# Both output accumulators in one PSUM bank, a quarter of a V chunk kept in the freed bank, and a shorter row norm in a two-layer attention decode kernel

## The chip, the cores and the metric

The kernel runs on one core of a Trainium2 chip. The metric is the device time of the launch in microseconds. The runs of the kernel before have a median of 1104.42 us (13 runs, 1099.99 to 1107.93); a run that was profiled took 1100.99 us.

## The reference, cut to what matters

Two layers are applied twice, with the same weights and the same caches in both passes. Layer A is attention of one new token per row over a cache; layer B is a small MLP. With a single position (S = 1) the four shifted groups of layer B are all zero, so its first two matrices drop out and only the part with `w3` and `w4` counts.

```python
B, Sq, D = 8, 1, 448;  Hq, Hkv, Sk, Dh = 16, 8, 4096, 256;  F = 1792    # bf16
# layer A
q = layernorm(x) @ wq                                  # 16 heads of 256
p = softmax(q . k_cache * Dh ** -0.5)                  # k_cache, v_cache: [8, 8, 4096, 256]
x = x + (p . v_cache) @ wo
# layer B, S = 1
y = layernorm(x);  x = x + y + gelu(layernorm(y) @ w3) @ w4
# ... then both layers once more
```

The caches hold 8 rows x 8 heads x 4096 x 256 x 2 bytes = 134 MB each. Pass 1 needs a query that depends on the end of pass 0 of the same row, so what isn't kept on the chip is read twice.

## The kernel before, in words

**Chunks and slots.** A task is one pass `ps` of one row `b` and one pair `gp` of key/value heads (4 pairs). It has four K chunks and four V chunks of 1 MB (128 partitions x 8 KB). SBUF has `NC = 15` places for chunks (`slots`). All chunk loads are issued on SP's queue by `emit_loads` (L671; L647 for two neighbouring K chunks at once), in the order in which the chunks are used, each as soon as a place is free. The engine that read a place last frees it: TensorE after the scores for K, TensorE after the product with the probabilities for V.

**What is kept.** Between a row's pass 0 and its pass 1, eleven chunks stay in their places (`kept`: all K of pairs 2 and 3, V chunks 1 to 3 of pair 3), so four of the 15 places are left for streaming. One more V chunk, `inner` (pair 2, V chunk 1), is saved in four PSUM banks: VectorE moves it as 128x512 uint32 transposes into `store` (`away`, L719) and later back into a place (`back`, L726). These twelve chunks of each row are loaded once only. The tasks are written out so that a row's two kept pairs come late in its pass 0, other rows' chunks stream while its chain runs, and pass 1 starts with the kept pairs.

**One chunk's work.** `items` is the hand-written order: K chunks of a task, interleaved with the V chunks of the task before it. For a K chunk VectorE transposes it in place (`transpose_k`, L684, three instructions), TensorE forms the scores into PSUM bank `sc` (L699), ScalarE takes the exponential (L708). `transpose_p` turns the probabilities (TensorE L735, ScalarE copy to `ptw` L742). For a V chunk `pv` (L754) adds 16 matmuls of 256 columns to an output accumulator in PSUM, one of two banks `o_banks`; `in_use` lists those taken. An accumulator serves two pairs of heads, then is drained.

**Side work.** The small work of a row is cut into generators, and the main loop calls `step` twice for each item, once ahead of the item's scores or `pv` and once at the item's end. `step` advances the first generator of each of three kinds in proportion to how far the item index is towards its due index.

- `half` drains an accumulator: sums of the exponentials (`z_cols`, VectorE L398 and L401, TensorE L409, VectorE L412), fold matrix `R` (L429), ScalarE copy of the accumulator to SBUF (L435), two small matmuls (L440), VectorE copy to `OT` (L444).
- `first_half` (pass 0, pairs 0 and 1) is `half` and the first part of the output projection (`add_cols`, L336). `chain` (pass 0, pairs 2 and 3) is `half`, the second part, the two additions to the residual `xT` (L465, L466), the MLP of the row (`mlp`, `norm` with `twice` set) and the query of pass 1 (`project_q`, `norm` again). `spread_q` then writes the query into a spread layout (L310).
- `first_last` and `last` drain pass 1. The last row's pairs 0 and 1 use another way (`pv_cols`), and the MLP of pass 1 is done for four rows at a time (`norm` with nb = 4).

`norm` for one row runs VectorE steps L210 to L224, one or two additions of epsilon (L245, L248), a power on GpSimd (L237), the centring (L251), and three scalings that write the bf16 operand `xb` (L262). The last 64 of the 448 features lie in the upper half of the partitions: `w3` and `wq` are stored with that tail split in two column halves, and `wblk` picks column 3 or 4 of `xb` for them.

PSUM has eight banks: `misc` (small results of many kinds at different columns), `sc`, two accumulators, four `store` banks.

Of the kernel before, what the change touches and what calls it, by code (L numbers as in the profile page):

```python
# [13 lines left out]
EPS = 1e-5  # L14
# [3 lines left out]
def kernel(  # L18
# [44 lines left out]
    kept = [(gp, 0, n) for gp in (GP - 1, GP - 2) for n in range(4)]  # L63
    kept += [(GP - 1, 1, n) for n in range(1, 4)]
    inner = (GP - 2, 1, 1)

    consts = ctx.enter_context(tc.tile_pool(name="consts", bufs=1))
    work = ctx.enter_context(tc.tile_pool(name="work", bufs=2))
# [43 lines left out]
    misc = psum.tile([128, 512], FP32, name="misc")  # L112
    ot_bank = misc[:, 256:320]
    sc = psum.tile([128, 512], FP32, name="sc")
    o_banks = [psum.tile([128, 512], FP32, name=f"o{n}") for n in range(2)]
    store = [psum.tile([128, 512], FP32, name=f"store{n}") for n in range(4)]
    for t in [sc] + o_banks:
        nc.vector.memset(t[:], 0.0)

    def room_ps(what, nb):  # L120

# [15 lines left out]
    ones = one[:].to_broadcast([128, 128])  # L137
    HTw = consts.tile([128, HC, Bn], BF16, name="HTw")
    nc.vector.memset(HTw[:], 0.0)
    nhalf = consts.tile([128, 1], FP32, name="nhalf")  # L140
    nc.vector.memset(nhalf[:], -0.5)
    xb = {}
# [29 lines left out]
    def wblk(t, cols, c, fc):  # L172

        if fc < 3:
            return t[:, fc * cols + 128 * c : fc * cols + 128 * c + 128], fc
        half = cols // 2
        if 128 * c < half:
            return t[:, 3 * cols + 128 * c : 3 * cols + 128 * c + 128], 3
        return t[:, 3 * cols + 128 * c - half : 3 * cols + 128 * c - half + 128], 4

# [12 lines left out]
    def norm(x, nb, twice):  # L193

        def room(name, shape, at):
            n = shape[0] * shape[1]
            if nb < Bn:
                t = chn.tile([128, n * MID], FP32, tag=name)  # L200
                ap = t[:, 0 : n * nb]
            else:
                ap = scratch(at, n * nb)
            return ap.rearrange("p (s f b) -> p s f b", s=shape[0], f=shape[1])

        def bc(ap):
# [36 lines left out]

        if twice:
            nc.vector.tensor_scalar(ve[:, 1], var, 0.0, EPS * EPS / (1 + EPS), ALU.max, ALU.add)  # L245
            if nb > 1:
                power(1, 2)
        nc.vector.tensor_scalar(ve[:, 0], var, 0.0, EPS, ALU.max, ALU.add)  # L248
        power(0, 2 if twice and nb == 1 else 1)
# [7 lines left out]
        parts = ((0, 128, 0, 0, 3, 0), (0, 64, 64, 3, 4, 3), (64, 128, 64, 3, 4, 4))  # L257
# [165 lines left out]
    def half(o_ps, zall, g8, OT):  # L423


        rz = yield from z_cols(zall, range(2 * g8, 2 * g8 + 2))

        R = chn.tile([128, 8], FP32, tag="R")
        nc.vector.tensor_mul(  # L429
            R[:].rearrange("p (g n) -> p g n", n=4),  # L430
            rz[:].rearrange("p n g -> p g n"),
            fold[:].rearrange("p (g n) -> p g n", n=4),
        )
        o_sb = chn.tile([128, Dh], FP32, tag="o_sb")
        nc.scalar.copy(o_sb[:], o_ps[:, 0:Dh])  # L435
        in_use.remove(o_ps)
        yield
        ot_ps = ot_bank[:, 32 * g8 : 32 * g8 + 16].rearrange("p (j h) -> p j h", j=2)
        for j in range(2):
            nc.tensor.matmul(  # L440
                ot_ps[:, j], o_sb[:].rearrange("p (i j) -> p j i", j=2)[:, j], R[:], start=True, stop=True
            )
        yield
        nc.vector.tensor_copy(OT[:, :, 8 * g8 : 8 * g8 + 8], ot_ps)  # L444
        yield
# [3 lines left out]
    def first_half(b, st):  # L449

        OT = work.tile([128, 2, Hq, 1], BF16, tag="OT", bufs=1)
        st["OT"] = OT
        yield from half(st["o", 0], st["z"], 0, OT[:, :, :, 0])
        yield from add_cols(
            y_room(1)[:, 0], lambda i: OT[:, i % 2, i // 2], wo_sb, range(NB2 // 2), 1
        )

    def chain(b, st):
        OT = st["OT"]
        yield from half(st["o", 1], st["z"], 1, OT[:, :, :, 0])  # L460
        yield from add_cols(
            y_room(1)[:, 1], lambda i: OT[:, i % 2, i // 2], wo_sb, range(NB2 // 2, NB2), 1
        )
        xs = xT[:, :, b : b + 1]
        nc.vector.tensor_add(xs, xs, y_room(1)[:, 0])  # L465
        nc.vector.tensor_add(xs, xs, y_room(1)[:, 1])  # L466
        yield from mlp(b, 1)
        qT = chn.tile([128, NB2], BF16, tag="qT2", bufs=2)
        yield from project_q(b, 1, qT[:].unsqueeze(2))
        state[1, b] = {"qT": qT}  # L470
# [75 lines left out]
    def inside(it):  # L546
        n, kv, c = it
        return (tasks[n][2], kv, c) == inner

    loads = [it for it in items if not (tasks[it[0]][0] == 1 and (stays(it) or inside(it)))]  # L550


# [79 lines left out]
    def emit_loads(most=None):  # L632
        n = 0
        while loads and places and n != most:
# [33 lines left out]
            else:  # L668
                src = rows.rearrange("(p x y) d -> x p (y d)", x=4, y=16)[c]
            if loads:  # L670
                nc.sync.dma_start(dst[:], src)  # L671
            else:
                for y in range(2):
                    nc.sync.dma_start(
# [69 lines left out]
            pt_ps.rearrange("p t k (a h) -> p a (t k) h", a=4),  # L744
        )

    def pv(o_ps, v, a, gp, begin):


        g = 2 * gp + a // 2  # L750
        for y in range(16):
            q = y % 4
            at = 128 * a + 8 * (4 * q + y // 4) + 6 - 2 * (g % 4)
            nc.tensor.matmul(  # L754
                o_ps[32 * q : 32 * q + 8, 0:256],
                ptz[:, at : at + 8],
                v[:, y * Dh : (y + 1) * Dh],
                start=(begin and y < 4),
                stop=(y >= 12),
                skip_group_check=True,  # L760
            )
# [39 lines left out]
            except StopIteration as e:  # L801
                return e.value

    gens, pairs_done, p_of, begun = [], {}, {}, set()
# [25 lines left out]
    for idx, it in enumerate(items):  # L830
# [65 lines left out]
        else:  # L896
# [23 lines left out]
            else:  # L920
                g8 = gp // 2
                if ("o", g8) not in st:
# [4 lines left out]
                pv(st["o", g8], slot, c, gp, begin=(ps, b, g8) not in begun)  # L927
                begun.add((ps, b, g8))
# [12 lines left out]
        if not (ps == 0 and stays(it)):  # L941
            if (ps, gp, kv, c) == (1, keep[-1], 0, 0):
                kept_place = p
            else:
                places.append(p)
        emit_loads()
        step(idx)
    while gens:
# [65 lines left out]
```

## Time and profile before

| what | value |
|---|---|
| median of 13 runs | 1104.42 us (1099.99 to 1107.93) |
| the profiled execution | 1100.99 us, span 1099.1 us |
| DMA | 448.90 MB, mean 408 GB/s |
| TensorE busy | 681.7 us (62%), granted clock 0.587 |
| VectorE busy | 586.3 us (53%) |
| ScalarE busy | 124.4 us (11%) |
| GpSimd busy | 16.3 us (1%) |
| chunk loads | 223 V of 1024 KB and 2 of 512 KB; 146 K of 1024 KB and 23 of 2048 KB |
| accumulators drained (L435) | 31 |

The busy shares are means over the whole span. The profile also gives the span in 40 slices of 27.5 us, the waits of each engine with what ended them, and a timeline; "SPq" in it is a DMA issue on SP's queue, and the text after "<-" in square brackets is what ended the engine's idle time before that row. All tables of stretches count from the span's start.

### The profile page before, as it was taken

What the parts mean: (1) busy time and instruction counts of PE and PEld (TensorE: products, weight loads), DVE (VectorE), ACT (ScalarE), POOL (GpSimd) and SP (SyncE); (2) the same over time, 40 slices, a digit from 0 to 9 for tenths busy, and PEclk for the clock granted to TensorE, in tenths of its full rate; (3) what the DMA queues carried; (4) which work ended last, traced back from release to release, by engine and by line L of the source; (5) the groups of instructions that cost most, each with busy time, mean ns of one, the idle gap of its engine ahead of it and who ended that gap; (6) DMA issues with size and microseconds to landing.
All of it is one profiled execution on the core that took longest, in us unless ns stands there. A gap on an engine that the chain in (4) does not pass through costs nothing. (4 is left out here: it accounts for less than half of the span.)

```text
span 1099.1 us, 32833 instructions
## 1 busy us (share of the span) xinstructions
PE 681.7 (62%) x15062; PEld 456.0 (41%) x15062; DVE 586.3 (53%) x1188; ACT 124.4 (11%) x362; POOL 16.3 (1%) x27
## 2 busy tenths in 40 slices
PE   3235668556864577446774477744777467867775
PEld 2123345334642355324542245522454245635554
DVE  5255564646356554556455564565637463576462
ACT  0001101110110011101020000200111101111110
POOL 0000000000000000000000000000000000000000
PEclk9996555655565556655565555755555555565575
DMA  9999999999999999999999999999999999999994
GB/s 361 396 426 420 419 397 420 420 413 409 417 423 420 405 416 422 424 419 398 419 422 422 421 399 418 423 422 415 409 419 421 419 405 420 421 414 403 417 418 186
DMA packets 62010, 448.90 MB, mean 408 GB/s; under 512 B 6568, under 2 KB 10544, under 8 KB 11312
## 3 DMA queue, kind: packets, MB, share of 16 engines
q1 hardware_dynamic: 61680, 446.42, 98.5%
q8 instruction: 118, 1.93, 0.7%
q10 hardware_dynamic: 192, 0.38, 0.1%
q14 instruction: 20, 0.16, 0.0%
HBM read 446.77 MB, written 0.01 MB: 407 GB/s over the span
## 5 line engine op out<-in xcount | busy, mean ns | idle before, releaser
L684 DVE STREAM_TRANSPOSE places<-places 128x512 uint32<-128x512 uint32 (+1 forms) x576 | 462.1, 858 | 282.3 <-DMA places<-in_A_k_cache_dram 274.1
L699 PE MATMUL sc<-places,qbd 128*8 128x128 bf16 (+1 forms) x6720 | 286.1, 313 | 226.3 <-DVE places L684 187.4
L754 PE MATMUL o<-places,ptw 128*8 128x256 bf16 x3968 | 246.3, 393 | 133.8 <-DMA places<-in_A_v_cache_dram 125.2
L699 PEld LDWEIGHTS <-qbd 128*8 128x8 bf16 x6720 | 164.4, 103 | 323.6 <-issue 146.7
L754 PEld LDWEIGHTS <-ptw 128*8 128x8 bf16 x3968 | 114.0, 111 | 181.4 <-issue 138.3
L708 ACT ACTIVATE p_n<-sc 128x256 bf16<-128x256 f32 x128 | 95.7, 748 | 806.0 <-PE sc L699 806.0
L287 PEld LDWEIGHTS <-wq_sb 128*128 128x128 bf16 x1152 | 35.9, 104 | 27.2 <-issue 18.9
L336 PEld LDWEIGHTS <-wo_sb 128*128 128x128 bf16 x1280 | 38.5, 103 | 19.7 <-issue 19.7
L310 DVE CAST qbd<-misc 32x64 bf16<-32x64 f32 x64 | 13.8, 216 | 55.8 <-PE misc L306 55.1
L287 PE MATMUL misc<-xb,wq_sb 128*128 128x1 bf16 x1024 | 34.5, 166 | 6.7 <-DVE xb L262 3.3
L336 PE MATMUL misc<-OT,wo_sb 128*128 128x1 bf16 x1024 | 34.4, 166 | 0.0
L708 ACT ACTIVATION_READ_ACCUMULATOR p_n<-sc 128x1 f32 x128 | 33.8, 264 | 0.0
L742 ACT CAST ptw<-misc 128x128 bf16<-128x128 f32 x64 | 17.5, 273 | 135.5 <-PE misc L735 75.8
L440 PEld LDWEIGHTS misc<-R,o_sb 128*128 128x128 f32 x124 | 28.0, 312 | 10.8 <-issue 8.7
L440 PE MATMUL misc<-R,o_sb 128*128 128x8 f32 x124 | 30.6, 358 | 0.4 <-ACT o_sb L435 0.3
L237 POOL TENSOR_TENSOR t<-t,nhalf 128x2 f32<-128x2 f32 (+2 forms) x20 | 14.0, 703 | 1069.5 <-DVE t L251 1069.5
L409 PE MATMUL misc<-zm,one 128*128 128x8 f32 (+1 forms) x66 | 18.1, 348 | 15.8 <-DVE zm L401 15.3
L726 DVE STREAM_TRANSPOSE places<-store 128x512 uint32<-128x512 uint32 x32 | 20.1, 685 | 11.3 <-PE sc L699 11.3
L409 PEld LDWEIGHTS misc<-zm,one 128*128 128x128 f32 x66 | 15.6, 293 | 22.1 <-issue 13.5
L354 PEld LDWEIGHTS <-w_sb 128*128 128x128 bf16 x560 | 17.2, 105 | 9.6 <-issue 9.4
L354 PE MATMUL misc<-xb,w_sb 128*128 128x1 bf16 (+1 forms) x560 | 18.5, 166 | 3.6 <-DVE xb L264 2.2
L719 DVE STREAM_TRANSPOSE store<-places 128x512 uint32<-128x512 uint32 x32 | 20.0, 694 | 1.0 <-DMA places<-in_A_v_cache_dram 0.9
(93 smaller groups left out, 227.3 us busy)
## 6 DMA issues: line engine op xcount, KB each, us to landing
places<-in_A_v_cache_dram SPq DMA_DIRECT2D x223, 1024.0 KB, 9.4
places<-in_A_k_cache_dram SPq DMA_DIRECT2D x146, 1024.0 KB, 10.7
places<-in_A_k_cache_dram SPq DMA_DIRECT2D x23, 2048.0 KB, 19.7
wo_sb<-in_A_wo_dram SPq DMA_DIRECT2D x1, 3584.0 KB, 28.5
wq_sb<-in_A_wq_dram SPq DMA_DIRECT2D x3, 1024.0 KB, 7.3
w_sb<-in_B_w_dram SPq DMA_DIRECT2D x1, 1568.0 KB
w_sb<-in_B_w_dram SPq DMA_DIRECT2D x3, 448.0 KB, 27.2
places<-in_A_v_cache_dram SPq DMA_DIRECT2D x2, 512.0 KB, 18.8
```

Of the source, the lines that this page charges most:

```text
L287: nc.tensor.matmul(q_ps[:, j * Hq + h, :], w, xbs(nb)[:, xi, :], start=(fc == 0), stop=(fc == 3),)
L336: nc.tensor.matmul(y_ps[:, fc, :], w[:, i, at : at + 128], rhs(i), start=start, stop=stop, skip_group_check=open is not None,)
L354: nc.tensor.matmul(h_ps[:, c * nb : c * nb + nb], w, xbs(nb)[:, xi, :], start=(fc == 0), stop=(fc == 3),)
L409: nc.tensor.matmul(z_ps, ones, zm[:], start=True, stop=True)
L440: nc.tensor.matmul(ot_ps[:, j], o_sb[:].rearrange("p (i j) -> p j i", j=2)[:, j], R[:], start=True, stop=True)
L684: nc.vector.transpose(w, w)
L699: nc.tensor.matmul(sc[32 * k : 32 * k + 8, 128 * x : 128 * (x + nx)], qbd[:, ep, gp].rearrange("p a h -> p (a h)"), v, start=(n == 0), sto ...
L708: nc.scalar.activation(p_sb[:, :, :, 2 * u : 2 * u + 2].rearrange("p t i x -> p x t i"), sc[:, 256 * u : 256 * u + 256].rearrange("p (x t ...
L719: nc.vector.transpose(store[n][:].bitcast(U32), slot[:].bitcast(U32)[:, 512 * n : 512 * n + 512])
L726: nc.vector.transpose(slot[:].bitcast(U32)[:, 512 * n : 512 * n + 512], store[n][:].bitcast(U32))
L742: nc.scalar.copy(ptw[:, :, :, 6:8], pt_ps.rearrange("p t k (a h) -> p a (t k) h", a=4),)
L754: nc.tensor.matmul(o_ps[32 * q : 32 * q + 8, 0:256], ptz[:, at : at + 8], v[:, y * Dh : (y + 1) * Dh], start=(begin and y < 4), stop=(y >= ...
```

## The change

1. **One bank for both accumulators.** `o0` and `o1` become the two halves (256 columns each) of one bank `o`. `pv` no longer starts its sum with the start flag. A matmul with zeros clears the whole bank at the beginning, and in `half` a VectorE memset clears the drained half after ScalarE's copy.
2. **A fifth store bank.** It keeps the first quarter (128 x 1024 bf16 = 2 KB per partition) of V chunk 0 of pair 3 (`part`). In pass 0 VectorE transposes it into the bank after the chunk's `pv`; in pass 1 VectorE transposes it back into the chunk's place one item ahead of its use, and the load of that chunk leaves the first quarter out.
3. **Shorter norm for one row.** With `twice` the two additions of epsilon are one instruction on two columns; in both kinds the first two of three scalings are one instruction with a constant mask `low`. For this, columns 3 and 4 of `xb` change roles, also in `wblk`.
4. **A moved addition.** The first of the two residual additions goes from `chain` to the end of `first_half`.

```diff
+    part = (GP - 1, 1, 0)
+    Q4 = 4 * Dh
...
-    o_banks = [psum.tile([128, 512], FP32, name=f"o{n}") for n in range(2)]
-    store = [psum.tile([128, 512], FP32, name=f"store{n}") for n in range(4)]
-    for t in [sc] + o_banks:
-        nc.vector.memset(t[:], 0.0)
+    o_both = psum.tile([128, 512], FP32, name="o")
+    o_banks = [o_both[:, 0:Dh], o_both[:, Dh : 2 * Dh]]
+    store = [psum.tile([128, 512], FP32, name=f"store{n}") for n in range(5)]
+    nc.vector.memset(sc[:], 0.0)
+    nc.tensor.matmul(o_both[:], ptz[:, 0:128], ptz[:, 0:512], start=True, stop=True)
...
+    low = consts.tile([128, 2, 4], FP32, name="low")
+    for k, v in enumerate((1.0, (1 + EPS) ** -0.5)):
+        nc.vector.memset(low[:, k], v)
+        nc.vector.memset(low[0:64, k, 3:4], 0.0)
+    eps2 = consts.tile([128, 2], FP32, name="eps2")
+    nc.vector.memset(eps2[:, 0:1], EPS)
+    nc.vector.memset(eps2[:, 1:2], EPS * EPS / (1 + EPS))
...
-        if twice:
-            nc.vector.tensor_scalar(ve[:, 1], var, 0.0, EPS * EPS / (1 + EPS), ALU.max, ALU.add)
-            if nb > 1:
+        if twice and nb == 1:
+            nc.vector.scalar_tensor_tensor(
+                ve[:, :, 0], var.to_broadcast([128, 2]), 0.0, eps2[:], ALU.max, ALU.add
+            )
+            power(0, 2)
...
+        if nb == 1:
+            nc.vector.scalar_tensor_tensor(
+                xbs(1)[:, 0:4, 0], xc[:, :, 0], rl, low[:, int(twice)], ALU.mult, ALU.mult
+            )
+            parts = parts[1:2]
...
-        nc.scalar.copy(o_sb[:], o_ps[:, 0:Dh])
-        in_use.remove(o_ps)
+        nc.scalar.copy(o_sb[:], o_ps)
+        nc.vector.memset(o_ps, 0.0)
+        in_use[:] = [t for t in in_use if t is not o_ps]
...
+        xs = xT[:, :, b : b + 1]
+        nc.vector.tensor_add(xs, xs, y_room(1)[:, 0])
...
-        nc.vector.tensor_add(xs, xs, y_room(1)[:, 0])
...
-                nc.sync.dma_start(dst[:], src)
+                z0 = Q4 if tasks[t][0] == 1 and halfway(it) else 0
+                nc.sync.dma_start(dst[:, z0:], src[:, z0:])
...
-                start=(begin and y < 4),
+                start=False,
...
+                if ps == 0 and halfway(it):
+                    nc.vector.transpose(store[4][:].bitcast(U32), slot[:, 0:Q4].bitcast(U32))
...
+        soon = items[idx + 1] if idx + 1 < len(items) else it
+        if tasks[soon[0]][0] == 1 and halfway(soon):
+            nc.vector.transpose(
+                slots[where[soon]][:, 0:Q4].bitcast(U32), store[4][:].bitcast(U32)
+            )
```

`halfway(it)` is true for the item that `part` names.

More of the change, by code (lines that the diff above doesn't have):

```diff
@@ L177, in wblk @@
         if 128 * c < half:
-            return t[:, 3 * cols + 128 * c : 3 * cols + 128 * c + 128], 3
-        return t[:, 3 * cols + 128 * c - half : 3 * cols + 128 * c - half + 128], 4
+            return t[:, 3 * cols + 128 * c : 3 * cols + 128 * c + 128], 4
+        return t[:, 3 * cols + 128 * c - half : 3 * cols + 128 * c - half + 128], 3
     def rows_to_cols(row, nb):
@@ L242, in power @@
             )
-        if twice:
-            nc.vector.tensor_scalar(ve[:, 1], var, 0.0, EPS * EPS / (1 + EPS), ALU.max, ALU.add)
-            if nb > 1:
+        if twice and nb == 1:
[3 more added lines that the diff above has]
+            power(0, 2)
+        else:
+            if twice:
+                nc.vector.tensor_scalar(
+                    ve[:, 1], var, 0.0, EPS * EPS / (1 + EPS), ALU.max, ALU.add
+                )
                 power(1, 2)
-        nc.vector.tensor_scalar(ve[:, 0], var, 0.0, EPS, ALU.max, ALU.add)
-        power(0, 2 if twice and nb == 1 else 1)
+            nc.vector.tensor_scalar(ve[:, 0], var, 0.0, EPS, ALU.max, ALU.add)
+            power(0, 1)
         xc = room("xc", (1, 4), 576)[:, 0]
@@ L256, in norm @@
         rl = rs[:, n - 1]
-        parts = ((0, 128, 0, 0, 3, 0), (0, 64, 64, 3, 4, 3), (64, 128, 64, 3, 4, 4))
+        parts = ((0, 128, 0, 0, 3, 0), (0, 64, 64, 3, 4, 4), (64, 128, 64, 3, 4, 3))
+        if nb == 1:
[3 more added lines that the diff above has]
+            parts = parts[1:2]
         for p0, p1, x0, f0, f1, to in parts:
@@ L548, in inside, with halfway @@
         return (tasks[n][2], kv, c) == inner
+    def halfway(it):
+        n, kv, c = it
+        return (tasks[n][2], kv, c) == part
     loads = [it for it in items if not (tasks[it[0]][0] == 1 and (stays(it) or inside(it)))]
@@ L745, in transpose_p, with pv @@
         )
-    def pv(o_ps, v, a, gp, begin):
+    def pv(o_ps, v, a, gp):
         g = 2 * gp + a // 2
@@ L754, in pv @@
             nc.tensor.matmul(
-                o_ps[32 * q : 32 * q + 8, 0:256],
+                o_ps[32 * q : 32 * q + 8, :],
                 ptz[:, at : at + 8],
                 v[:, y * Dh : (y + 1) * Dh],
-                start=(begin and y < 4),
+                start=False,
                 stop=(y >= 12),
@@ L802, in run @@
                 return e.value
-    gens, pairs_done, p_of, begun = [], {}, {}, set()
+    gens, pairs_done, p_of = [], {}, {}
     def add_gen(kind, b, g, at, until, total):
@@ L926 @@
                     in_use.append(st["o", g8])
-                pv(st["o", g8], slot, c, gp, begin=(ps, b, g8) not in begun)
-                begun.add((ps, b, g8))
+                pv(st["o", g8], slot, c, gp)
                 if ps == 0 and inside(it):
                     away(slot)
+                if ps == 0 and halfway(it):
+                    nc.vector.transpose(store[4][:].bitcast(U32), slot[:, 0:Q4].bitcast(U32))
             if c == 3:
@@ L945 @@
                 places.append(p)
+        soon = items[idx + 1] if idx + 1 < len(items) else it
+        if tasks[soon[0]][0] == 1 and halfway(soon):
+            nc.vector.transpose(
+                slots[where[soon]][:, 0:Q4].bitcast(U32), store[4][:].bitcast(U32)
+            )
         emit_loads()
```

## The prediction

> **What bounds the kernel now.** I read the page's slices first, then its queue table, then tables of stretches, then the timeline of one row, and last the list of waits.
>
> ```profile
> span 1099.1 us, 32833 instructions
> ...
> DMA  9999999999999999999999999999999999999994
> GB/s 361 396 426 420 419 397 420 420 413 409 417 423 420 405 416 422 424 419 398 419 422 422 421 399 418 423 422 415 409 419 421 419 405 420 421 414 403 417 418 186
> ...
> q1 hardware_dynamic: 61680, 446.42, 98.5%
> ```
>
> The DMA engines are full in every slice but the last, and nearly all they move is q1's chunk loads. No compute engine is above 62%. So the time is bytes over rate, plus a head and a tail. The GB/s row has a level, about 420, and dips to about 400 that return every 131 us, once for each row. The stretches of one row show where:
>
> ```profile
> core 0: us, PE busy (x) PEld busy (x) DVE busy (x) ACT busy (x) POOL busy (x), PEclk, DMA share, GB/s
> 372.00:388.00 16.00, 11.89 (x253) 8.11 (x257) 9.86 (x26) 1.49 (x4) 0.70 (x1) 0.50 0.99 387
> 388.00:416.00 28.00, 21.36 (x480) 14.70 (x473) 13.04 (x33) 2.46 (x8) 0.55 (x1) 0.50 1.01 420
> 436.00:500.00 64.00, 30.95 (x642) 19.45 (x638) 34.75 (x50) 7.08 (x20) 0.00 (x0) 0.61 1.01 421
> ```
>
> 436 to 500 is the comfortable part: kept places have been freed, many loads are queued (median issue to landing there 20 to 22 us). 372 to 416 is the tight part, with four places for streaming: issue to landing falls to 7.3 us for K and 8.1 for V. For its first 16 us the rate is 387 instead of 420, a loss of 16 x (1 - 387/420) = 1.3 us. The timeline shows the loop of one K place there:
>
> ```profile
> 379.15 2.43 DVE L684 STREAM_TRANSPOSE places<-places 128x1024 uint32<-128x1024 uint32 x3 [2.72 <-DMA places<-in_A_k_cache_dram]
> ...
> 382.06 0.33 SPq L671 DMA_DIRECT2D places<-in_A_k_cache_dram  x1
> ...
> 389.32 1.25 DVE L684 STREAM_TRANSPOSE places<-places 128x1024 uint32<-128x1024 uint32 x1 [1.94 <-DMA places<-in_A_k_cache_dram]
> ```
>
> K lands at 379.15, its place is free and reloaded at 382.06, the new chunk lands at 389.32. That is 10.17 us for a turn in which four places move 4.19 MB: 412 GB/s, against 9.98 us at 420. The loop is at the edge: a release that comes later there can cost DMA time, elsewhere not.
>
> **The change part by part.**
>
> *The bytes.* Eight rows load 128 x 2 KB less: 2.097 MB. At 420 GB/s this is 4.99 us. It counts in full only if the shorter load runs at the same rate. The Trainium skill ("DMA: Bandwidth & Descriptors", section Bandwidth) speaks against it: it says to batch loads to 1 MiB or more for 75% of peak, and the eight loads fall to 768 KB with 6 KB per partition. The trace's nearest low case is 24 to 44 us, where weights come in smaller pieces: 380 GB/s. If the eight loads (6.29 MB) ran at 380, they would cost 6.29/0.380 - 6.29/0.420 = 1.6 us and leave 3.4 us. But what decides here is that other loads are queued behind; whole chunks run at 420, not at 75% of anything. I take 4.9, with ends 3.4 and 5.0.
>
> *Transposes of the quarter.* Eight out, eight back, each like a row of the kept chunk:
>
> ```profile
> L719 DVE STREAM_TRANSPOSE store<-places x32: 682/684/727, 92.8 to 966.0; 128x512 uint32<-128x512 uint32 x32
> L118 DVE MEMSET o<- x2: 485/485/485, 2.8 to 3.3; 128x512 f32 x2
> ```
>
> 16 x 0.68 = 11 us of VectorE. The one out waits for the chunk's landing and `pv` takes 1.07 us on the same chunk, so the place is freed as late as before; it lies about 15 us ahead of the tight part, where several loads are queued. The one back lies at the row's start (about 425 us in this row): VectorE then waits 4.98 us at L444 for TensorE, and `pv` of that chunk starts at 427.25. The transpose back should end by about 426.4. Cost nothing; with that 0.8 us cover gone, up to 0.7 us a row. On SP's queue the shorter load keeps its place; no DMA is added.
>
> *Memsets.* 31 in `half`, half as wide as the L118 row: 0.25 us (at most 0.49), 8 us of VectorE. What counts is whom they hold up. All `pv` now write one bank. The Trainium skill ("PSUM — Partial Sum Buffer", section "PSUM bank collisions raise a hardware error") says that two engines must not touch the same bank and quadrant at once, so copy and memset have to be ordered against every `pv`, also that of the other accumulator. The list of waits shows that programs here are ordered so for disjoint columns:
>
> ```profile
> PE misc L287 <- ACT ptw L742: 3.2, 8, 0.4
> ```
>
> L287 writes columns 384 to 415 of `misc`, L742 reads columns 0 to 127, and TensorE waits. So I count this. Were every drain on the path, 31 x (0.38 copy + 0.25 memset + some 0.1 of hand-over) = 23 us would be added. The timeline says what lies on the path. The first drain in the tight part:
>
> ```profile
> 371.43 0.38 ACT L435 COPY o_sb<-o 128x256 f32<-128x256 f32 x1
> ...
> 371.89 0.57 PE L409 MATMUL misc<-zm,one 128*128 128x8 f32 x2
> ...
> 372.39 1.02 PE L754 MATMUL o<-places,ptw 128*8 128x256 bf16 x16
> 372.50 0.21 DVE L412 RECIPROCAL rz<-misc 128x8 f32<-128x8 f32 x1 [0.76 <-PE misc L409]
> 372.74 0.17 DVE L429 TENSOR_TENSOR R<-rz,fold 128x8 f32<-128x8 f32 x1
> ...
> 373.46 0.33 SPq L671 DMA_DIRECT2D places<-in_A_v_cache_dram  x1
> 373.94 1.25 DVE L684 STREAM_TRANSPOSE places<-places 128x1024 uint32<-128x1024 uint32 x1 [1.03 <-DMA places<-in_A_k_cache_dram]
> ```
>
> Copy and memset come after L429 in the code. `step` runs ahead of `pv` in an item, and `chain` makes 38 steps in about 18 items, so each call does one: sums, L409, then L412 with copy and memset, all ahead of this `pv` in program order. The copy can still run at 371.43. The memset runs at 372.95 to 373.2 in VectorE's idle 1.03 us, so the K transposes at 373.94 aren't held. `pv` then starts at 373.25, not 372.39: 0.86 us late, and so is the V load at 373.46. Behind it L440 ends at 375.2, when the next scores can start anyway. V loads have about 0.8 us of room (8.1 us to landing where K needs 7.3), so I book 0.1 us a row, ends 0 and 0.6: 0.8 us over eight rows. The tight part's second drain (L412 at 401.89) delays its `pv` by 0.4 us, the V release after it has more room; nothing. The other drains lie where loads queue up.
>
> *Norm and the moved addition.* For a row: L245 and L248 (0.22 us together, overlapped) become one instruction of about 0.22 (L224's row); the three L262 (0.69 us) become two, about 0.45, twice: 0.5 us of VectorE a row. The K transposes come ahead of L262 in most rows, and wait for DMA; gain nothing, at best 0.2 us a row where they don't. The addition (L465, 0.12 us) moves to the comfortable part, one step after its matmuls. Start: two memsets of 0.485 us go, six of some 0.06 and one matmul come; loads run already. `pv` keeps its 3968 matmuls; the flag costs nothing.
>
> *Sum.* Against the profiled execution, 1100.99 (span 1099.1 and 1.9 around it): -4.9 + 0.8 = -4.1, so 1096.9. That execution lies 3.4 us below the median of the runs; the forecast is for the median: 1104.4 - 4.1 = 1100.3.
>
> **The rivals.**
>
> *Slower: the drain blocks VectorE in the tight loop.* If the copy lands behind the `pv` of its item in program order, it waits for it in the shared bank, and VectorE waits for the copy. At the second drain: `pv` ends 403.26, copy and memset to 403.95, so the norm's steps start 1.8 us late, its scalings end near 405.7, and the K transposes behind them, due at 404.51, start 1.2 us late in a loop without room. With 0.2 us at the first drain this is 1.4 us a row: 8 x 1.4 - 4.9 = +6.3, 1110.7. It decides from 0.61 us a row (4.9/8) and is measurably slower from 0.89. For it: the loop's 10.17 us. Against: two of three steps put the copy ahead of `pv`, as worked out above.
>
> *No gain: the transfer is hidden.* The saved load lies at the row's start (issued 411.89, landed 420.0), where places are still few. DMA gets 0.61 us ahead, but releases from 418 to 433 follow the chain of queries, scores and exponentials, not the DMA; if loads run dry before the places come free, the 0.61 us is spent waiting: 0 to -1 us, 1103.9. For it: the 7 us from landing of that chunk to its `pv` at 427.25. Against: the rate at the row's start stays near 420 in the slices.
>
> *The shorter load doesn't pay:* 6 KB packets at 8 KB's price would give nothing; at 380 GB/s 1101.8 with the 0.8 us. It falls within the range.
>
> **How the numbers follow.** About 0.2% (2.2 us) is what a measurement of this kernel can tell from no change, so faster is below 1102.2, slower above 1106.6. Main case 0.66 (1098.8 to 1102), hidden or half hidden 0.15 (1102 to 1105), drain in the loop 0.17 (1106 to 1112), more gain than the bytes by shorter dips 0.02. The main case with a few of the hidden makes faster 0.70, the rest of the hidden same 0.14, slower 0.16. The range from 1098.5 to 1105.5 leaves out the slower case and a little below.
>
> **What would show it.** Right: 2.1 MB less in the queue table, eight V loads of 768 KB, 420 GB/s level unchanged, dips of 16 us with 380 or more, span about 4 us shorter, everything after the first row start shifted by 0.6 us a row. The V issue after each first drain comes 0.9 us later relative to the K landing before it; VectorE rows of 0.25 us for the memset stand right behind L429. Wrong: the tight stretches fall below 410 over their whole length, or K transposes there start with an idle time ended by ScalarE's copy; or the GB/s falls at the row starts by as much as the bytes saved.

## The result, and the profile after

The changed kernel took 1097.81 us (median of 11 runs, 1095.76 to 1101.78) beside 1104.66 us of the kernel before on the same chip (48 runs, 1099.99 to 1110.79): a ratio of 0.9942 [0.9926, 0.9959] (the two medians alone would give 0.9938; the ratios with their 95% intervals are used from here on). Because one comparison of this kernel is uncertain by some 2 us, the unchanged "after" was compared three more times, among the experiments:

| comparison of the changed kernel | median, us | ratio to before, 95% |
|---|---|---|
| first | 1097.81 | 0.9942 [0.9926, 0.9959] |
| `e5_again` | 1097.19 | 0.9943 [0.9915, 0.9972] |
| `e13_again` | 1099.35 | 0.9968 [0.9946, 0.9991] |
| `e18_third` | 1099.32 | 0.9951 [0.9928, 0.9973] |

Weighted by their intervals the four give 0.9950 ± 0.0011, which is 5.5 ± 1.2 us off 1104.4. The lowest executions, 1095.6 to 1096.5 us after and 1099.75 to 1100.1 before, are only about 4.1 us apart. The forecast was 1100.3 with a low end of 1098.5. The direction came out as predicted; the 1097.81 us of the first comparison lie 0.7 us below that end. The gain was larger than the 4.1 us of the sum by 2.3 us in the first comparison and by 1.4 us in the four together.

The page of the profiled execution (1095.60 us), its span, its slices, the queue of the chunk loads and the issues of the shortened load:

```profile
span 1093.8 us, 32866 instructions
...
GB/s 359 395 425 420 420 399 418 420 415 408 416 423 419 401 416 421 422 420 404 415 421 424 421 403 418 422 422 418 406 420 420 419 405 419 421 414 408 413 419 188
...
q1 hardware_dynamic: 61680, 444.32, 98.6%
...
places<-in_A_v_cache_dram SPq DMA_DIRECT2D x8, 768.0 KB, 7.3
```

The queue moved 2.10 MB less in the same number of packets, so the eight loads run in smaller packets, and the level of the slices is still 420 with a dip for each row. The mean rate over the span is 408 GB/s in both kernels, and 2.10 MB at 408 GB/s is 5.1 us of the 5.3 us by which the span is shorter. In this pair of profiles, then, the time came out of the bytes, and the rate did not pay for it. The stretches of the row that the prediction showed (busy time by engine, granted clock, DMA share, rate), and after them two row starts, where the quarter comes back:

```profile
core 0: us, PE busy (x) PEld busy (x) DVE busy (x) ACT busy (x) POOL busy (x), PEclk, DMA share, GB/s
372.00:388.00 16.00, 12.47 (x270) 8.21 (x270) 9.48 (x23) 1.49 (x4) 0.70 (x1) 0.50 0.99 386
388.00:416.00 28.00, 20.45 (x462) 14.15 (x460) 13.07 (x33) 2.62 (x8) 0.55 (x1) 0.50 1.01 419
436.00:500.00 64.00, 28.62 (x605) 17.77 (x592) 36.38 (x56) 7.24 (x20) 0.00 (x0) 0.66 1.01 421
410.40:436.40 26.00, 21.23 (x478) 13.94 (x470) 13.28 (x27) 3.98 (x12) 0.00 (x0) 0.57 1.02 421
541.10:567.10 26.00, 21.29 (x450) 13.42 (x442) 13.42 (x28) 4.05 (x12) 0.00 (x0) 0.59 1.02 418
```

386, 419 and 421 stand against 387, 420 and 421 before: the tight part with its four places is no slower. The row starts run at 421 and 418 (422 and 419 in the same stretches before), so the saved load is not spent waiting there. The row starts themselves can be read from the tile moved back from the four old store banks:

```profile
L755 DVE STREAM_TRANSPOSE places<-store x32: 673/675/718, 178.0 to 1036.5; 128x512 uint32<-128x512 uint32 x32
```

The first one stands at 178.0 (178.1 before), the last at 1036.5 (1040.9 before). That is 4.3 us over the seven row starts between them, 0.61 us each, which is what 0.262 MB take at 420 GB/s (0.62 us).

The drain did what the prediction's program order said. The timeline of the first drain in the tight part (start, duration, engine and line):

```profile
370.72 0.38 ACT L457 COPY o_sb<-o 128x256 f32<-128x256 f32 x1
...
372.03 0.17 DVE L451 TENSOR_TENSOR R<-rz,fold 128x8 f32<-128x8 f32 x1
372.25 0.27 DVE L458 MEMSET o<- 128x256 f32 x1
372.57 1.03 PE L783 MATMUL o<-places,ptw 128*8 128x256 bf16 x16 [0.82 <-DVE o L458]
...
373.21 2.43 DVE L713 STREAM_TRANSPOSE places<-places 128x1024 uint32<-128x1024 uint32 x3 [0.69 <-DMA places<-in_A_k_cache_dram]
...
373.64 0.33 SPq L700 DMA_DIRECT2D places<-in_A_v_cache_dram  x1
```

The copy runs ahead, the memset stands right behind L451, `pv` waits 0.82 us for it, and the V load is issued 0.43 us after the K transposes begin, where it was issued 0.48 us ahead of them before: 0.9 us later. But VectorE still idles 0.69 us for the K chunk, so the loop of K is not held. Over all drains, the list of waits shows what the shared bank costs each engine (total us, times, longest):

```profile
ACT o_sb L457 <- PE o L783: 31.6, 12, 8.3
...
DVE o L458 <- ACT o_sb L457: 10.4, 8, 2.3
...
PE o L783 <- DVE o L458: 9.3, 12, 1.5
```

These are 51 us of waits on three engines, none of which is in the list of before, in a kernel that became faster.

The second drain of the tight part is the place with least room. Its timeline:

```profile
401.21 0.17 DVE L451 TENSOR_TENSOR R<-rz,fold 128x8 f32<-128x8 f32 x1
401.43 0.27 DVE L458 MEMSET o<- 128x256 f32 x1
...
402.93 0.22 DVE L276 SCALAR_TENSOR_TENSOR xb<-t,low 128x4 bf16<-128x4 f32 x1 [0.66 <-POOL t L247]
403.19 0.21 DVE L284 TENSOR_SCALAR xb<-t 64x1 bf16<-64x1 f32 x1
403.61 2.43 DVE L713 STREAM_TRANSPOSE places<-places 128x1024 uint32<-128x1024 uint32 x3 [0.20 <-DMA places<-in_A_k_cache_dram]
```

Memset, the rest of the norm and the K transposes of the next chunk stand in one line on VectorE, with 0.20 us left before the chunk lands. Before the change the same place had 0.28 us:

```profile
403.50 0.73 DVE L262 TENSOR_SCALAR xb<-t 128x3 bf16<-128x3 f32 x3 [0.66 <-POOL t L237]
404.51 2.43 DVE L684 STREAM_TRANSPOSE places<-places 128x1024 uint32<-128x1024 uint32 x3 [0.28 <-DMA places<-in_A_k_cache_dram]
```

The memset adds 0.27 us to that line and the shorter norm takes about a quarter of a microsecond out of it: 0.73 us for three scalings, 0.47 us from the start of L276 to the end of L284. So the memset stands ahead of both tight drains' K transposes. At the first drain that is so in all eight rows, with 0.69 to 1.10 us of idle time left; at the second in five rows, with 0.20 to 0.48 us left (0.27 to 0.35 us before). In the other three rows no memset stands there.

### The profile page after: what moved, and what is told of

It is laid out like the page before. It is cut to its first block, busy times and chain, and to the rows that moved or that the text cites. A ratio compares the mean times of both kernels' runs of the same rounds, so it can differ in the third digit from the quotient of the medians.

```text
span 1093.8 us, 32866 instructions
## 1 busy us (share of the span) xinstructions
PE 681.0 (62%) x15063; PEld 456.3 (42%) x15063; DVE 598.8 (55%) x1215; ACT 126.1 (12%) x362; POOL 16.3 (1%) x27
```

## The experiments

The theory: the gain is the bytes, and memset and shorter norm settle against each other on VectorE. The rivals: the gain comes from something else (the norm, the start, the moved addition); the drain costs what was booked and the bytes bring more; the drain costs nothing anyway. An interval of a single run is about ± 2 to 3 us, so most parts were tried both alone and taken out.

**The quarter taken out.** The chunk is loaded whole, and nothing is kept in the fifth bank; all else is as after.

```diff
-                z0 = Q4 if tasks[t][0] == 1 and halfway(it) else 0
-                nc.sync.dma_start(dst[:, z0:], src[:, z0:])
+                nc.sync.dma_start(dst[:], src)
...
-                    nc.vector.transpose(store[4][:].bitcast(U32), slot[:, 0:Q4].bitcast(U32))
...
-            nc.vector.transpose(
-                slots[where[soon]][:, 0:Q4].bitcast(U32), store[4][:].bitcast(U32)
-            )
```

> The changed kernel without its second part: the chunk is loaded whole, no quarter goes to the fifth store bank; shared accumulator bank, memsets and shorter norm stay. Theory A (the bytes are all, 5.0 us; drains and norm cost and give nothing): within 0.5 us of the kernel before, ratio 1.000. Theory B (the prediction's sum: the drains cost 0.1 us a row): +0.8 us, 1.0007. Theory C (the gain beyond the bytes comes from the shorter norm or from the drains): about 1.5 us faster than before, ratio 0.9985.

Measured: 1104.98 us, ratio 1.0007 [0.9985, 1.0029]. Without the quarter the gain is gone: bank, memset, norm and moved addition together are worth +0.8 ± 2.4 us.

**The norm alone,** put into the kernel before (the functions as in the diff of the change, nothing else).

> The kernel before with the shorter norm alone. Theory A: no difference, within 0.5 us. Theory C: 1 to 2 us faster, since VectorE steps in the four-place stretch shorten the loop of a K place; the dips' GB/s rises above 387 in the profile. Old and new norm differ by 0.5 us of VectorE a row, so no more than 4 us in any case.

Measured: 1104.76 us, ratio 1.0014 [0.9988, 1.0039]: +1.5 ± 2.8 us. Alone it brings nothing that can be measured.

**The shorter load alone.** The kernel before, with the quarter neither kept nor loaded: the bytes of the change without its VectorE and PSUM work. What the quarter adds to the product is left out.

```diff
-                nc.sync.dma_start(dst[:], src)
+                z0 = 4 * Dh if tasks[t][0] == 1 and (tasks[t][2], kv, c) == (GP - 1, 1, 0) else 0
+                nc.sync.dma_start(dst[:, z0:], src[:, z0:])
```

> The kernel before, with the one edit that pass 1 loads the chunk without its first quarter; that quarter keeps what the place held, so this part of the product is left out of the computation. No shared bank, no memset, no transposes of the quarter, old norm. Theory A (bytes are all that moves the time, the drains cost nothing net): as the changed kernel, 5.0 us below before, ratio 0.9955, lowest execution near 1095.5. If the drains cost 0.8 us in the changed kernel: this one is 0.8 us faster than it. Theory C' (norm, bank or moved addition also bring about 1 us): this one is 1 us slower than the changed kernel.

> The kernel before with only the shorter load (the quarter keeps what the place held, left out of the computation), beside the changed kernel. Bytes alone: the two agree within 1 us, both near 0.9955. Otherwise this one is 2 us or more slower than the changed kernel, near 0.9966.

Measured: 1098.98 and 1099.28 us, ratios 0.9966 [0.9948, 0.9984] and 0.9966 [0.9945, 0.9988], together -3.8 ± 1.5 us. So the bytes alone bring most of it.

**The shorter load with the new norm.** Both edits above in the kernel before.

> The shorter load and the shorter norm on the kernel before; two accumulator banks, no memset, no transposes of the quarter (its part left out of the computation as in the run before). If the norm brings what the bytes don't: about 2 us faster than the shorter load alone, ratio 0.994. If the norm is worth nothing where no memset stands ahead of the K transposes: equal to the shorter load alone within 1 us.

Measured: 1098.74 us, 0.9955 [0.9936, 0.9974]: -5.0 ± 2.1 us, not to be told from the shorter load alone.

**The norm taken out.** The kernel after with the old `norm` (two additions of epsilon, three scalings).

> The changed kernel with the old norm. Theory N (the shorter norm pays for the memset: in the second drain of the four-place stretch both stand ahead of the K transposes, whose idle time was 0.27 us before and 0.21 after): the idle time there falls to about 0, K releases come up to 0.1 us late, 0 to 2 us slower than the changed kernel, ratio 0.994 to 0.997. If the shorter norm were worth nothing even beside the memset, the idle time would stay above 0.15 us and the time the same.

> The changed kernel with the old norm, beside the changed kernel. In the first run of it the idle time ahead of the K transposes at the second drain was 31 ns in four of five rows, and the ratio 0.9979 (interval 0.9955 to 1.0003). Theory N (the norm's 0.22 us pays for the memset's 0.27): 2 to 4 us slower than the changed kernel again. If that was chance: within 1 us of it.

Measured: 1099.64 us, 0.9979 [0.9955, 1.0003], and 1101.65 us, 0.9978 [0.9956, 1.0000]. Together 0.9979 ± 0.0016 or -2.4 ± 1.8 us, which is 3.1 ± 2.1 us slower than after by the ratios. Where the two ran side by side on one chip (`e16_old_norm_again` and `e13_again`) the ratios are 0.9978 and 0.9968, 1.1 us apart, which is within the scatter. The timeline of `e16_old_norm_again` at the second drain of a row shows where the norm is missing:

```profile
531.83 0.27 DVE L446 MEMSET o<- 128x256 f32 x1
...
533.33 0.72 DVE L272 TENSOR_SCALAR xb<-t 128x3 bf16<-128x3 f32 x3 [0.66 <-POOL t L247]
534.08 2.43 DVE L701 STREAM_TRANSPOSE places<-places 128x1024 uint32<-128x1024 uint32 x3
```

The three scalings take 0.72 us, and the K transposes follow with no idle time. In the five rows with a memset at this drain the idle time ahead of these transposes is 0.31 us once and 0.03 us four times in this profile; after the change it is 0.20 to 0.48 us, before 0.27 to 0.35 us. So the memset with the old norm uses the room up, and the new norm gives it back. But using it up cost no time that these profiles show. The tile moved back at the row starts tells how long the rows take:

```profile
L743 DVE STREAM_TRANSPOSE places<-store x32: 671/673/717, 177.9 to 1035.8; 128x512 uint32<-128x512 uint32 x32
```

That is 857.9 us for the old norm in `e16_old_norm_again` (857.7 in `e10_old_norm`), against 858.5 us after the change. Both profiles caught the fastest execution of their run (1095.81 and 1095.22 us; the profile of after took 1095.60). What sets the old norm back in the slower executions, if anything does, is not in these traces.

**A dearer drain.** The memset three times instead of once.

```diff
-        nc.vector.memset(o_ps, 0.0)
+        for _ in range(3):
+            nc.vector.memset(o_ps, 0.0)
```

> The changed kernel with the accumulator's memset done three times in a row: 0.54 us more behind L451 in each of 31 drains; the first drain of the four-place stretch then starts its pv about 1.4 us later than the kernel before did, and the K transposes there start up to 0.1 us late. If the V loads have only the 0.8 us of room that the prediction gave them: 8 x 0.5 = 4 us slower than the changed kernel. Theory A (more room, the drain is off the path): within 1 us of the changed kernel.

Measured: 1107.25 us, 1.0031 [1.0010, 1.0053], which is 8.9 ± 2.7 us slower than after. The timeline of its two tight drains (first, then second):

```profile
371.69 1.07 DVE L459 MEMSET o<- 128x256 f32 x3
372.71 2.43 DVE L714 STREAM_TRANSPOSE places<-places 128x1024 uint32<-128x1024 uint32 x3
...
402.17 1.07 DVE L459 MEMSET o<- 128x256 f32 x3
...
404.73 0.21 DVE L284 TENSOR_SCALAR xb<-t 64x1 bf16<-64x1 f32 x1
404.97 2.43 DVE L714 STREAM_TRANSPOSE places<-places 128x1024 uint32<-128x1024 uint32 x3
```

The two more memsets put 0.80 us on VectorE in each drain. Both idle times ahead of the K transposes (0.69 and 0.20 us after the change) are gone. What is over the room is 0.80 - 0.69 + 0.80 - 0.20 = 0.7 us in this row. Five rows have both drains; with 0.1 us for each of the other three this estimate gives 3.9 us, against the 8.9 ± 2.7 us measured and 6.7 us over seven row starts in this profile (178.3 to 1043.5). So it accounts for about half, and the rest was not located. Without any room all 31 drains would have cost 31 x 0.80 = 25 us. A drain that stays within the idle time ahead of the K transposes showed no price here, and one that went beyond it did.

**The drain later.** Copy and memset one step further on, and so behind the `pv` of their item: the order in the prediction's slower rival.

```diff
+        yield
         nc.scalar.copy(o_sb[:], o_ps)
         nc.vector.memset(o_ps, 0.0)
         in_use[:] = [t for t in in_use if t is not o_ps]
-        yield
```

> The changed kernel with the drain's copy and memset one step later, that is behind the pv of the same item in program order in the first drain of the four-place stretch, ahead of the small matmuls. This is the place that the slower rival of the prediction supposed. Rival's price: in the first drain pv ends 373.6, copy and memset to 374.3, K transposes 1.1 us late in a loop that has no room: with the second drain 1.2 to 1.4 us a row, 8 x 1.3 = 10 us slower than the changed kernel, ratio to before about 1.004. Theory A (the loop has room of about a microsecond that the queued loads give): under 2 us slower than the changed kernel, ratio to before 0.995 to 0.997.

Measured: 1102.46 us, 0.9993 [0.9972, 1.0013], 4.7 ± 2.6 us slower than after. Timeline of its first tight drain:

```profile
372.65 0.37 ACT L458 COPY o_sb<-o 128x256 f32<-128x256 f32 x1 [1.94 <-PE o L783]
...
373.15 0.27 DVE L459 MEMSET o<- 128x256 f32 x1 [1.06 <-ACT o_sb L458]
373.33 2.40 DVE L713 STREAM_TRANSPOSE places<-places 128x1024 uint32<-128x1024 uint32 x3
```

The chain is the one the rival named: the copy waits for `pv`, the memset for the copy, and the K transposes stand behind the memset with no idle time. Here they start about when they would have anyway, and the rival had estimated 0.2 us at this drain. Its total, 1.4 us a row, was too much: it would have put the rival 10.4 us above the prediction's sum, not 4.7. Most of it, 1.2 us, was for the second drain, and there this run doesn't have the rival's order: the K transposes start at 404.07 after 1.15 us of idle time, and the memset comes behind them at 406.56. Where in the rows the 4.7 us go was not settled: most of what its profile loses, it loses in one row of the eight, at slices of 373 and 399 GB/s.

**The drain off VectorE.** ScalarE clears the half instead.

```diff
-        nc.vector.memset(o_ps, 0.0)
+        nc.scalar.mul(o_ps, o_sb[:], 0.0)
```

> The changed kernel with the clearing of the drained half on ScalarE (the copy in SBUF times zero, 0.38 us behind the copy) in place of the VectorE memset. In the first drain of the four-place stretch copy and clearing end at about 371.5 on the changed kernel's clock, ahead of the pv at 371.7, so the pv starts on time and VectorE has its 1.0 us of idle time back. If the drain still costs something in the changed kernel: 1 to 3 us faster than it, ratio 0.991 to 0.994. If the one memset lies wholly within the room: the same as the changed kernel.

Measured: 1098.90 us, 0.9963 [0.9947, 0.9978]. Timeline of its first tight drain:

```profile
369.89 0.38 ACT L457 COPY o_sb<-o 128x256 f32<-128x256 f32 x1
370.30 0.39 ACT L458 ACTIVATE o<-o_sb 128x256 f32<-128x256 f32 x1
370.85 1.02 PE L783 MATMUL o<-places,ptw 128*8 128x256 bf16 x16
...
372.40 2.43 DVE L713 STREAM_TRANSPOSE places<-places 128x1024 uint32<-128x1024 uint32 x3 [1.04 <-DMA places<-in_A_k_cache_dram]
```

`pv` is on time again, without a wait, and the idle time of VectorE is back at the 1.03 us that it had before the change. The time isn't better than after: the ratios put this run 1.4 ± 2.1 us above it, and its tile moved back at the row starts stands at 177.9 to 1036.6, 858.7 us, against 858.5 us after. So the memset on VectorE with the new norm beside it, the wait of `pv` for the drain (0.82 us in the timeline of after) and the late V load cost nothing that these runs can measure.

**`pv` ahead of the step.** For V items the side work's `step` goes behind `pv`, unless a drain is in its first steps.

```diff
-            step(idx)
+            first = final or any(e["n"] < 4 for e in gens)
+            if first:
+                step(idx)
...
                 pv(st["o", g8], slot, c, gp)
+                if not first:
+                    step(idx)
```

> The changed kernel with the step of the side work put behind pv in V items, except while a drain is in its first steps. In the four-place stretch V places are then freed 0.5 to 1 us earlier in most turns. If late V releases are what costs the 1.0 to 1.4 us at each onset: up to 5 us faster, ratio near 0.990. If the K loop sets the rate there: no difference to the changed kernel within 1 us.

Measured: 1101.46 us, 0.9981 [0.9960, 1.0002]. Freeing V places earlier brought nothing, and the run is 3.4 ± 2.6 us slower than after; why was not looked into.

**More bytes saved, early chunk.** Only the last quarter of the same chunk is loaded: 6.29 MB less than before instead of 2.10. What the second and third quarter add to the product is left out.

```diff
-                z0 = Q4 if tasks[t][0] == 1 and halfway(it) else 0
+                z0 = 3 * Q4 if tasks[t][0] == 1 and halfway(it) else 0
```

> The changed kernel, but the load of the chunk in pass 1 fetches only its last quarter; quarters two and three keep what the place held, so this part of the product is left out of the computation. 8 x 512 KB = 4.19 MB less than the changed kernel, 6.29 MB less than before. Theory A (every byte counts at 420 GB/s): 10.0 us below the changed kernel, 15.0 us below before, ratio 0.9864. Rival (the saved time is spent waiting for places at the row's start): the second and third quarter give less than half, ratio above 0.991, and SP's issues at the row start meet an empty queue, with GB/s below 400 in the slices there.

Measured: 1097.09 us, 0.9946 [0.9914, 0.9979], so -6.0 ± 3.6 us: the further 4.19 MB, 10 us of DMA time at 420 GB/s, gave nothing that can be measured. Stretches of 26 us around three of its row starts:

```profile
core 0: us, PE busy (x) PEld busy (x) DVE busy (x) ACT busy (x) POOL busy (x), PEclk, DMA share, GB/s
409.80:435.80 26.00, 21.52 (x498) 14.45 (x490) 13.46 (x28) 4.43 (x13) 0.00 (x0) 0.60 1.01 410
539.30:565.30 26.00, 21.40 (x451) 13.47 (x444) 13.46 (x28) 4.04 (x12) 0.00 (x0) 0.59 1.00 399
671.90:697.90 26.00, 20.82 (x451) 13.47 (x448) 13.24 (x27) 4.33 (x13) 0.00 (x0) 0.58 1.01 410
```

410, 399 and 410 stand against 421 and 418 in the same stretches after the change: the loads run out of free places, as the prediction's hidden-transfer rival described it. It is wrong for the first quarter and right for more.

**More bytes saved, later chunk.** The same three quarters, of a chunk that is used later in the row.

```diff
-    part = (GP - 1, 1, 0)
+    part = (GP - 2, 1, 3)
...
-                z0 = Q4 if tasks[t][0] == 1 and halfway(it) else 0
+                z0 = 3 * Q4 if tasks[t][0] == 1 and halfway(it) else 0
```

> As the run that loaded only the last quarter, but of another chunk: V chunk 3 of pair 2, used seven items later in pass 1, when places have come free. Quarters two and three keep what the place held, so this part of the product is left out of the computation. 6.29 MB less than before. Theory S (what stops further bytes from paying is the shortage of places at the row's start, not the bytes): the full 15 us come, ratio 0.9864 to 0.989, and the loss in 26 us around a row's start falls from 1.1 us a row to 0.3. Rival (any bytes beyond the first quarter are lost, since another wait takes over everywhere): ratio 0.994 as with the early chunk.

Measured: 1092.30 us, 0.9893 [0.9864, 0.9922]: -11.8 ± 3.2 us of the 15.0 us in 6.29 MB. So it is the place in the row that decides. In its profile a good part of the rest is lost in one stretch near the end:

```profile
960.00:1000.00 40.00, 27.07 (x624) 17.48 (x627) 26.53 (x51) 4.54 (x13) 0.70 (x1) 0.59 0.96 374
```

40 us at 374 GB/s instead of 421 are 40 x (1 - 374/421) = 4.5 us.

**The quarter of the later chunk, kept as in the change,** once with the memset and once with ScalarE's clear (only `part`, and in the second also the clear, is edited).

> The changed kernel with the kept quarter taken from V chunk 3 of pair 2 instead of V chunk 0 of pair 3; nothing is left out. Theory S: the loss around the row's start, 0.37 us a row in the changed kernel, goes back to the 0.27 of before, 0.8 us in all, ratio 0.9935 to 0.995. Rival (place does not matter for one quarter): no difference to the changed kernel within 0.5 us.

> The changed kernel with the kept quarter taken from V chunk 3 of pair 2 and the clearing of the drained half on ScalarE, everything computed. If the two small costs that are left in the changed kernel, some 0.8 us around the row starts and up to 1 us at the drains, both go: 6 us below before, ratio 0.9945 or less, loss around the row starts 1.7 us. If they were within chance: the same as the changed kernel, 0.995.

Measured: 1099.17 us, 0.9959 [0.9936, 0.9982], and 1098.85 us, 0.9961 [0.9937, 0.9985]. Neither is better than the change as it is. With one quarter saved the place doesn't matter yet; no version that computes everything was found to beat the change clearly.

**The change again.**

> The changed kernel once more, unaltered, for the size of the gain and a second profile. Theory A (bytes only): 5.0 us below before, ratio 0.9955. Prediction's sum: 4.1 us, 0.9963. Theory C' (the first comparison's 6.4 us is real, because shorter loads also ease the four-place stretch): 0.994. In the profile, theory A expects the time lost against 421.5 GB/s to be as before: about 9 us at the eight onsets of the four-place stretch, 2 to 3 us around the row starts.

> The changed kernel, on one chip with the next three. If its gain is the bytes alone (the run with only the shorter load gave 0.9966, interval 0.9948 to 0.9984): 0.996 or above. If the first size is real and comes from the edits together: 0.9943.

> The changed kernel beside it on the same chip: 0.995, between 0.9938 and 0.9962, the weighted mean of its three comparisons.

Their times are in the first table.

## Why the prediction was right in direction, and its sum too small

All differences to before, in us with 95% intervals, from the ratios above ("drain" stands for the shared bank with its memset, and what else of the change comes with it):

| | bytes not saved | quarter not loaded |
|---|---|---|
| old drain, old norm | 0 | -3.8 ± 1.5 |
| old drain, new norm | +1.5 ± 2.8 | -5.0 ± 2.1 |
| new drain, old norm | not run | -2.4 ± 1.8 |
| new drain, new norm (the last column is the change) | +0.8 ± 2.4 | -5.5 ± 1.2 |

*The bytes: right.* Along each full row the second column less the first is -3.8 ± 1.5, -6.5 ± 3.5 and -6.3 ± 2.7; weighted, -4.7 ± 1.2. Booked were 4.9. The rule of the Trainium skill that spoke against it ("DMA: Bandwidth & Descriptors", section Bandwidth: loads of 1 MiB or more) did not bear on this queue, where other loads stand beside them: the eight loads land in 7.3 us and the level stays at 420.

*The transposes of the quarter: right.* The one back runs at 424.49 to 425.17 and its `pv` starts at 426.02, in VectorE's wait for TensorE, as placed; the row starts keep their rate. `e1_no_quarter`, which drops them with the saved load, loses about what the bytes are worth.

*The drain: this is the step that failed.* Order, wait of `pv` (0.82 us, worked out 0.86) and late V load (0.9 us) came as written, and the memset took 0.27 us for 0.25. The cost drawn from them, +0.8 us for V loads that are short of room, did not come. In the pair of profiles a row takes 0.61 us less, of the 0.62 us that the bytes are worth, and `e11_act_clear`, with `pv` and V load on time again, takes 858.7 us over seven row starts where after takes 858.5 (857.9 with the memset and the old norm). So the term measured about zero in the profiles, and without it the sum is the bytes alone, -4.9 us and 1099.5. The medians are too coarse to say the same by themselves: with the old norm the drain comes to +1.4 ± 2.3 us (-2.4 less -3.8). The second drain, booked at nothing for its later `pv`, turned out to be the one with little room, on VectorE.

*The range: too narrow below.* Its low end lay 1.8 us under the forecast and came from the ends of the terms; the uncertainty of one comparison of this kernel, 1.9 us in the first, takes that up alone. The four comparisons together give 1104.4 - 5.5 = 1098.9, inside the range; the first one's 6.4 us lies in the scatter of the four. That it fell outside is in part chance.

*The norm: open.* "Gain nothing, at best 0.2 us a row where they don't" rests on K transposes that come ahead of the scalings and wait for DMA. They come ahead of L262 in one of a row's two norms; in the other, at the second drain, the scalings stand ahead of them, but the transposes did still wait, 0.27 us or more. Alone the norm brought nothing (+1.5 ± 2.8, and -1.2 ± 2.6 beside the shorter load). Beside the memset, which takes that wait away, it gives it back: 0.27 us in and 0.25 us out, on the same engine ahead of the same transposes. The traces show this exchange of idle time, which the prediction, weighing each edit against the kernel before, did not see. That it is worth time is not shown: 3.1 ± 2.1 us by the ratios, 1.1 us where both ran side by side on one chip, nothing in the profiles.

*What stays open.* 4.9 against 5.5 ± 1.2 us is no difference. Whether drain and norm together bring a little (the change less the shorter load alone is -1.7 ± 1.9 us) is not settled by these runs, nor is what part the moved addition and the start have, which were not run alone.

*The rivals.* The slower one needed the copy behind `pv`; in the change it is ahead at both tight drains, and with it behind at the first the price was 4.7 ± 2.6 us, about what the bytes bring. The hidden transfer came true only for bytes beyond the first quarter.

## What to carry to other kernels

Follow a delay to the end before booking a price for it: here `pv` and a V load left 0.8 to 0.9 us late, and 51 us of new waits stood in the list, yet the rows took no longer. For each place where a small cost is added, look up the idle time that ends with a DMA behind it on that engine; while the cost stays within that idle time it may be free, and beyond it the time went up. Weigh the parts of a change against the kernel that they make together, because one edit can use up the idle time that another gives back. And draw a range no narrower than the scatter of one comparison. Bytes saved in a kernel bound by DMA count in full only while places are free for the next load, so choose what to keep on the chip by where in the row its load would have stood.

## What the runs showed of the hardware that was not expected

- Loads with packets of 6 KB lost nothing of the rate that can be seen: 7.3 us from issue to landing and a level of 420 GB/s; the whole chunks before took 7.3 to 8.1 us in the tight part.
- Clearing 128x256 f32 in PSUM took 0.27 us on VectorE and 0.39 us on ScalarE.
- Executions of one kernel spread more than most edits move it: 1099.99 to 1110.79 us for the kernel before. The profile of `e9_before_short` caught an execution of 1105.82 us, 9.6 us above the lowest of the same kernel (1096.24), so its rows can't be compared with those of the other profiles. Its slices show that the loss is in the dips:

```profile
GB/s 359 396 424 421 419 400 416 420 407 410 410 422 421 397 413 417 426 419 403 411 412 423 421 398 410 421 424 416 394 412 421 415 397 411 420 395 381 410 420 177
```

The level of 420 to 424 is that of the other kernels. The dips of the last six rows go to 397, 403, 398, 394, 397 and 381, where in the profile of after the same slices have 401, 404, 403, 406, 405 and 408, and slices beside them fall to 410 to 413, one to 395. They are the stretches with few loads queued. Why one execution loses more there than the next is open.
